# A router beside the experts: token ids from 10 + 4 matrix products instead of 40, and search products planned later

## The chip, the cores and the metric

The kernel runs on one core of a Trainium2 chip. A core has a tensor engine (PE; its weight loads are listed as PEld), a vector engine (DVE), a scalar engine (ACT), GpSimd (POOL) and a queue engine (SP) that only issues DMAs. Each executes its own instructions in the order in which they were written, and waits for the others by semaphores. The metric is the device time of one execution in microseconds.

## The reference

Attention over 8 batches of 8 heads (576 tokens, head size 64) with a bias from a running sum; its output is 4608 tokens of 512 numbers. Then a mixture of 8 experts: tokens and experts are paired greedily by descending logit, each expert takes 576 tokens, and each token passes through the two layers of its one expert.

```
logits = x @ w_gate                       # 4608 x 8
order = np.argsort(-logits.flatten())
for idx in order:
    tok, e = idx // E, idx % E
    if assigned[tok] >= 0 or counts[e] >= cap:
        continue
    assigned[tok] = e
    counts[e] += 1
for e in range(E):
    mask = assigned == e
    h = np.maximum(x[mask] @ w1[e], 0.0)
    out[mask] = h @ w2[e]
```

## The kernel before, in words

**Stages.** Attention comes first. After it come a router, which finds the greedy assignment without sorting, and the experts; the router's first search step (L886) starts at 358 us of the profiled execution. Router and experts are written into the same instruction streams.

**The router.** Tokens lie as 128 partitions by 40 columns. The router works in eight phases, j = 0 to 7; each settles which expert fills up next and which tokens go to it. Phases 0 to 6 search a threshold in seven steps, one digit of the key each. A step is a chain to and fro between DVE and PE: comparisons into `ge` (L886), ten products into `psa` that count per expert (L909), a copy `ca` (L913), four products into `psb` that add up over the partitions with the selecting matrices `qb` (L918), a comparison `pe` (L921), one product (L923), a maximum `jc` (L926), the next key `wd` (L930). Phase 7 has no search. Each phase then gives every chosen token its place among the 576 (products L982 and L983, a scan), and one product (L1003) updates the counts.

**Ids from places.** `Router.places` turns places into the list of token ids that the gather needs. A place is split into two digits of base 32 (`db`). `ol` marks for each token the lower digit (128 partitions, 10 groups, 32 values, 4 columns), `ob` the upper one (18 values). `rv` holds two factors of the id times `ob`: in its first half a number for the token's column, in its second the partition. Summing `ol` transposed times `rv` over all tokens leaves at [lower digit, upper digit] the id that has this place. The sum runs over 128 partitions and 40 columns; before, it is made of 40 products that accumulate, each with 32 columns of weights taken from `ol` at a step of 4 and 36 moving columns from `rv` at a step of 4. DVE copies the 32 x 36 sums to `pf` and makes `ids` of them. Then POOL gathers the expert's tokens (`xg`, L1097, five indirect DMAs), and SP transposes them by DMA (`xT`, L1104); for expert 0 PE does it (L1112).

**The experts.** Expert j has 96 large products in its first layer (512 columns, L1163), each with a short one behind it (64 columns, L1167), and 112 large ones in its second (L1237, L1234); for expert 0 the first layer is split and has more. ACT and DVE turn sums into `hT` and split each float32 weight, loaded by SP into `wst`, into a high part (ACT, L1132) and a low one (DVE, L1135). The loads start when the router has named the expert. Results go out by indirect DMAs of POOL (L1217).

**What sets the order.** A planner (`Plan`) takes tasks, each with an engine, a duration in microseconds, the tasks that it needs, a priority and the buffers that it takes. It simulates the engines with these durations and always writes out the task that could start first, lower priority number first among equals. A slot of a `Ring` of buffers comes free when the planned end of its last user has passed. The durations and `slack` are part of the kernel; they decide the order alone and make nothing wait at run time:

```
def _when(self, x, e):
    t = max(x.ready + x.slack, self.free[e])
```

Only the router's products inside `phase` carry slack, from the table `SLACK` by `min(j, 2)`: none in phase 0, 0.15 us in phase 1, 0.3 us in phases 2 to 7. The router's tasks have priority 0, the experts' products 2 + j. So the planner fills PE with expert products until a router product's planned time has come, and writes it there. At run time PE reaches it in that order, and if its operand is not there yet, PE waits with everything behind it.

Of the kernel before, what the change touches and what calls it, by code (L numbers as in the profile page):

```python
# [9 lines left out]
F32 = mybir.dt.float32  # L10
F16 = mybir.dt.float16
BF = mybir.dt.bfloat16
I32 = mybir.dt.int32
AF = mybir.ActivationFunctionType
# [10 lines left out]
CAP = 576  # L25
# [179 lines left out]
class Attention:  # L205
# [26 lines left out]
    def buf(self, name):  # L232
        return Buf(self.r[name])
# [465 lines left out]
WS1, WS2 = 32.0, 64.0  # L699
YSC = 1.0 / (VS * WS1 * WS2)  # L700
NEG = -1.0e30
SLACK = (0.0, 0.15, 0.3)
NONE = 1.0e9
NT = 8 * S

# [1 line left out]
class Router:  # L707
# [109 lines left out]
    def rings(self):  # L817
        w, o = self.w, self.out
        R = lambda pool, shape, dt, name, n: Ring([pool.tile(shape, dt, name=f"{name}{i}") for i in range(n)])
        self.r = dict(  # L820
            ge=R(w, [128, NC_ // 4, J, 4], F16, "ge", 2), y=R(w, [128, NC_], F32, "y", 2),
            ca=R(w, [128, 4, E], F16, "ca", 2), pe=R(w, [128, E], F16, "pe", 2), wd=R(w, [128, NC_], BF, "wd", 2),
            jc=R(w, [128, 8], F32, "jc", 2), jm=R(w, [128, 8], F32, "jm", 2), t8=R(w, [128, 7, E], F32, "t8", 2),
            gg=R(w, [128, 2, NC_], F32, "gg", 2), gv=R(w, [128, 2, NC_], F32, "gv", 2), vi=R(w, [128, 4], I32, "vi", 2),
            tm=R(w, [128, NC_, E], F32, "tm", 1), cp=R(w, [128, E], F16, "cp", 2),
            sel=R(w, [128, 2, E], F32, "sel", 2), v1=R(w, [1, 1], F32, "v1", 1), va=R(w, [128, E], F32, "va", 1),
            vstar=R(o, [128, 1], F32, "vstar", 3), ei=R(o, [1, 1], I32, "ei", 3),
            X=R(o, [128, 2, NC_], F16, "X", 3), Y=R(o, [128, 2, NC_], F32, "Y", 3), ids=R(o, [128, 5], I32, "ids", 4),
            Z=R(w, [128, 2, NC_], F32, "Z", 1), si=R(w, [128, NC_], I32, "si", 1), d=R(w, [128, 2, NC_], I32, "d", 1),
            db=R(w, [128, 2, NC_ // 4, 4], BF, "db", 1), ob=R(w, [128, NC_ // 4, CAP // 32, 4], BF, "ob", 1),  # L830
            rv=R(w, [128, 2, NC_ // 4, CAP // 32, 4], BF, "rv", 1), ol=R(w, [128, NC_ // 4, 32, 4], BF, "ol", 1),
            pf=R(w, [32, 2, CAP // 32], F32, "pf", 1),
            A=Ring([self.ps.tile([128, 512], F32, name="psa")]), B=Ring([self.ps.tile([128, 512], F32, name="psb")]),
            C=Ring([self.ps.tile([128, 512], F32, name="psc")]))

# [182 lines left out]
    def places(self, pl, info, X, Y, placed, prio):  # L1018

        nc, v = self.nc, self.nc.vector  # L1020
        buf = lambda name: Buf(self.r[name])
        chain = [placed]

        def V(dur, f, **k):
            chain[0] = pl.add("v", dur, f, chain[:1], prio=prio, **k)
            return chain[0]
        Z, si, d, db, ob, rv, ol, C, pf, ids = (buf(n) for n in ("Z", "si", "d", "db", "ob", "rv", "ol", "C", "pf", "ids"))
        nb = CAP // 32

        V(0.241, lambda: v.scalar_tensor_tensor(Z.t, Y.t, -1024.0, X.t, op0=OP.add, op1=OP.mult), takes=[Z], uses=[X, Y])  # L1030
# [15 lines left out]
              takes=[] if h else [ol], uses=[db] + ([ol] if h else []))  # L1046

        def f_pi():
            pi = C.t[0:32, 0:2 * nb].rearrange("p (a b) -> p a b", a=2)
            for q in range(10):  # L1050
                for c in range(4):
                    nc.tensor.matmul(pi, ol.t[:, q, :, c], rv.t[:, :, q, :, c], start=(q == c == 0),
                                     stop=(q == 9 and c == 3))
        chain[0] = pl.add("t", 1.25, f_pi, chain[:1], prio=prio, takes=[C], uses=[ol, rv])
        info["pi"] = chain[0]
        V(0.16, lambda: v.tensor_copy(pf.t, C.t[0:32, 0:2 * nb].rearrange("p (a b) -> p a b", a=2)), takes=[pf], uses=[C])
        for a in range(4):
            n = 5 if a < 2 else 4
            V(0.157, lambda a=a, n=n: v.scalar_tensor_tensor(
# [270 lines left out]
```

## Time and profile before

| | us |
|---|---|
| three runs, median | 839.58 |
| three runs, lowest and highest | 838.43, 843.65 |
| profiled execution, its own time | 842.17 |
| its span, first to last instruction | 840.3 |
| mean granted clock of PE over the span, share of full | 0.944 |
| busy: PE, DVE, ACT, POOL | 744.2, 606.2, 377.1, 349.7 |
| first and last of the products L1052 | 385.1, 681.0 |

An engine's busy time is the union of its instructions. A product counts as busy to its modelled end, about 0.17 us after the next one has started, so the time that a product takes in a stream is the distance between starts, or the time of a whole group in the chain of waits divided by its count. In the chain a row is a start, a time and a group that was on the chain. In the view in order of time a row is a start, a duration from the first start to the last end, the engine, the line, what is written and read, the shape and the count, and in square brackets the engine's idle time before it with what ended it. "issue" means that no wait that the profile shows ended then, "remote" a release that it cannot assign.

### The profile page before, as it was taken

Reading aid. Unit: us, or ns where it says so; the run is one execution under the profiler, and the core shown is the slowest. Engines: PE = TensorE matmul, PEld = TensorE weight load, DVE = VectorE, ACT = ScalarE, POOL = GpSimd, SP = SyncE. Lnnn points to the kernel's source line nnn. Section 1 sums busy time; section 2 is a strip of 40 time slices with the busy share of each in tenths; the row PEclk is TensorE's granted clock in tenths of the full one; section 3 lists DMA queues with packets and bytes.
Section 4 is the critical chain, followed back from the end, with each engine's and each line's share of the span. In section 5 each row is a group of like instructions: output and inputs, shape, how many; then the busy total and the mean of one; then the engine's idle time right before and its main releaser. Section 6 shows DMA issues by size and latency. Waiting matters only on the chain.

```text
span 840.3 us, 23577 instructions
## 1 busy us (share of the span) xinstructions
PE 744.2 (89%) x9267; PEld 470.0 (56%) x9267; DVE 606.2 (72%) x1992; ACT 377.1 (45%) x716; POOL 349.7 (42%) x423
## 2 busy tenths in 40 slices
PE   4299999999989999625999999998989999999995
PEld 1167778877768877512754545444545545454442
DVE  7679999999999997367887888886878854240110
ACT  2367877877768766403433323232323324231110
POOL 5178878878878887302023031222030150201011
PEclk7589999999999999856999999999999999999998
DMA  4956757675666511105258394848285494510001
GB/s 140 284 135 166 220 162 226 191 225 154 191 174 200 144 31 59 58 1 194 66 162 209 113 225 146 155 170 185 77 208 150 152 253 150 136 51 29 29 14 44
DMA packets 85317, 119.31 MB, mean 142 GB/s; under 512 B 40726, under 2 KB 57238, under 8 KB 85206
## 3 DMA queue, kind: packets, MB, share of 16 engines
q1 hardware_dynamic: 79318, 98.93, 42.5%
q0 software_dynamic: 5888, 18.88, 7.5%
q8 instruction: 72, 1.18, 0.6%
q14 instruction: 39, 0.32, 0.1%
HBM read 71.67 MB, written 19.10 MB: 108 GB/s over the span
## 4 chain that ended last, share of the span: by engine, by line
PE 43%; issue 21%; DVE 17%; POOL 4%; DMA 2%; another core or an unknown queue 1%; ACT 1%; POOLq 0%; DVEq 0%; SPq 0%; ACTq 0%
PE psm L1163 12%; PE psm L1237 9%; DVE scr L442 6%; DVE QK L381 3%; PE pst L514 2%; PE pst L515 2%; POOL out_dram L1217 2%; PE pss L473 2%; PE po L587 2%; PE po L589 2%; PE psn L1167 2%; PE po L588 2%; PE psa L909 2%; PE psm L1234 1%; POOL xg L1097 1%
## 5 line engine op out<-in xcount | busy, mean ns | idle before, releaser
L527 POOL TENSOR_TENSOR R<-P 128x512 f16<-128x512 f32 (+1 forms) x224 | 237.1, 1082 | 46.1 <-ACT P L525 44.9
L1163 PE MATMUL psm<-xT,w1p 128*128 128x512 f16 (+1 forms) x876 | 197.6, 356 | 0.0
L1237 PE MATMUL psm<-w2p,hT 128*128 128x512 f16 x768 | 175.9, 380 | 0.0
L1217 POOL DMA_INDIRECT out_dram<-y,ids x40 | 42.2, 1055 | 262.9 <-ACT y L1248 204.0
L1167 PE MATMUL psn<-xT,w1p 128*128 128x64 f16 x768 | 142.7, 193 | 0.0
L525 ACT ACTIVATE P<-pst 128x512 f32<-128x512 f32 (+1 forms) x224 | 117.7, 548 | 52.3 <-PE pst L517 25.6
L442 DVE CUSTOM_DVE_ANT_0 scr<-pss,mS 128x512 bf16<-128x512 f32 (+3 forms) x256 | 124.1, 485 | 13.6 <-PE pss L473 2.9
L1163 PEld LDWEIGHTS <-w1p 128*128 128x128 f16 x876 | 80.0, 98 | 83.9 <-issue 5.8
L1237 PEld LDWEIGHTS <-hT 128*128 128x128 f16 x768 | 70.2, 98 | 81.2 <-issue 3.2
L587 PE MATMUL po<-V,P 128*128 128x65 f16 x960 | 111.0, 196 | 2.3 <-DVE xp L608 1.8
L514 PE MATMUL pst<-QK 70*128 70x64 f16 (+4 forms) x512 | 106.7, 251 | 6.8 <-DMA QK<-mt 6.5
L589 PE MATMUL po<-V,R 128*128 128x65 f16 x960 | 111.0, 194 | 0.0
L588 PE MATMUL po<-Vl,P 128*128 128x64 f16 x960 | 110.8, 193 | 0.0
L515 PE MATMUL pst<-QK 128*128 128x64 f16 (+4 forms) x512 | 106.4, 251 | 0.0
L1097 POOL DMA_INDIRECT xg<-xs,ids x40 | 42.9, 1072 | 135.1 <-DVE w L809 43.6
L1183 ACT ACTIVATE hT<-psm 128x512 f16<-128x512 f32 x64 | 38.2, 597 | 133.9 <-PE psm L1163 99.2
L587 PEld LDWEIGHTS <-P 128*128 128x128 bf16 x960 | 90.2, 98 | 8.6 <-issue 6.1
L588 PEld LDWEIGHTS <-P 128*128 128x128 bf16 x960 | 89.7, 99 | 7.5 <-issue 3.7
L473 PE MATMUL pss<-QK 67*128 67x512 f16 (+3 forms) x256 | 73.4, 310 | 20.9 <-DVE mr L442 13.1
L589 PEld LDWEIGHTS <-R 128*128 128x128 f16 x960 | 89.7, 97 | 0.0
L1185 DVE SCALAR_TENSOR_TENSOR hT<-psm,hT 128x512 f16<-128x512 f32 x64 | 44.0, 687 | 51.6 <-ACT hT L1183 51.5
L1248 ACT ACTIVATE y<-psm 128x512 f32<-128x512 f32 x32 | 19.1, 597 | 130.2 <-PE psm L1237 121.0
(199 smaller groups left out, 1427.1 us busy)
## 6 DMA issues: line engine op xcount, KB each, us to landing
QK<-QK SPq DMA_DIRECT2D x120, 144.0 KB
wst<-in_w_dram SPq DMA_DIRECT2D x32, 512.0 KB
wst<-in_w_dram SPq DMA_DIRECT2D x64, 256.0 KB
rv<-in_v_dram SPq DMA_DIRECT2D x16, 576.0 KB
raw<-in_q_dram SPq DMA_DIRECT2D x15, 576.0 KB
raw<-in_k_dram SPq DMA_DIRECT2D x15, 576.0 KB
xs<-xp SPq DMA_DIRECT2D x8, 1024.0 KB
xs<-xp SPq DMA_DIRECT2D x8, 128.0 KB
```

The lines of the kernel that those rows point to most:

```text
L442: return pl.add("v", dur, lambda: nc.vector.tensor_tensor_reduce(scr.t[:, :n], ps(), mask, 1.0, init() if init else -3e38, OP.add, OP.max, ...
L473: nc.tensor.matmul(ps.t[:, :n], F()[:, q0:q0 + 128], F()[:, k0:k0 + n], start=True, stop=True)
L514: nc.tensor.matmul(ps[:, c0:c0 + n], F()[:, ks:ks + 128], F()[:, q:q + n], start=True, stop=False)
L515: nc.tensor.matmul(ps[:, c0:c0 + n], G()[:, ks:ks + 128], G()[:, q:q + n], start=False, stop=not diag)
L525: e = pl.add("a", n / 1200 + 0.171, lambda: nc.scalar.activation(P.t[:, c0:c0 + n], ps.t[:, :n], AF.Exp, scale=1.0 / YS), [x] + fresh, pri ...
L527: sub = lambda eng: eng.tensor_tensor(R.t[:, c0:c0 + n], P.t[:, c0:c0 + n], strided_hi(P.t)[:, c0:c0 + n], op=OP.subtract)
L587: nc.tensor.matmul(o[:, i], H[:, c:c + 128], V.t[:, pr, sl], start=f, stop=False)
L588: nc.tensor.matmul(o[:, i, 0:64], H[:, c:c + 128], Vl.t[:, pr, sl], start=False, stop=False)
L589: nc.tensor.matmul(o[:, i], R.t[:, c:c + 128], V.t[:, pr, sl], start=False, stop=l)
L1163: nc.tensor.matmul(ps[:, tiles[0]:tiles[-1] + 1] if len(tiles) > 1 else ps[:, tiles[0]], lhs(f, c, a), xT.t[:, tiles[0]:tiles[-1] + 1, 4 * ...
L1167: nc.tensor.matmul(pt.t[:, 64 * f:64 * f + 64], lhs(f, c, a), xT.t[:, 4, 4 * b + c, 0:64], start=s, stop=e)
L1237: nc.tensor.matmul(py.t, hT.t[:, f, a, 128 * i:128 * i + 128], w2p.t[:, f, b], start=f == 0 and k == 0, stop=f == 7 and k == 2)
```

## The change

`places` gets ten products in the place of forty. Each takes a whole group of four token columns: 128 columns of weights, which are 32 lower digits for each of the 4 columns, and 144 moving ones, which are 2 halves, 18 upper digits and 4 columns. Their sum also holds combinations of two different token columns, which mean nothing. ACT copies the 128 x 144 sums to float16 (`pc`, a new buffer). Then four products, one for each column of a group, select with 32 columns of `qb` the rows that belong to that column, take every fourth column of `pc`, and add the four up into 32 x 36 sums at another place of the same bank of PSUM. The planned durations are 0.63 us for the ten, 0.3 us for the copy and 0.12 us for the four, where the forty had 1.25 us. The third entry of `SLACK` goes from 0.3 to 0.45.

```diff
-SLACK = (0.0, 0.15, 0.3)
+SLACK = (0.0, 0.15, 0.45)
...
-            pf=R(w, [32, 2, CAP // 32], F32, "pf", 1),
+            pf=R(w, [32, 2, CAP // 32], F32, "pf", 1), pc=R(w, [128, CAP // 4], F16, "pc", 1),
...
         def f_pi():
-            pi = C.t[0:32, 0:2 * nb].rearrange("p (a b) -> p a b", a=2)
             for q in range(10):
-                for c in range(4):
-                    nc.tensor.matmul(pi, ol.t[:, q, :, c], rv.t[:, :, q, :, c], start=(q == c == 0),
-                                     stop=(q == 9 and c == 3))
-        chain[0] = pl.add("t", 1.25, f_pi, chain[:1], prio=prio, takes=[C], uses=[ol, rv])
+                nc.tensor.matmul(C.t[:, 0:8 * nb], ol.t[:, q].rearrange("p i c -> p (i c)"),
+                                 rv.t[:, :, q].rearrange("p a b c -> p a (b c)"), start=q == 0, stop=q == 9)
+        x = pl.add("t", 0.63, f_pi, chain[:1], prio=prio, takes=[C], uses=[ol, rv])
+        x = pl.add("a", 0.3, lambda: nc.scalar.activation(pc.t, C.t[:, 0:8 * nb], AF.Copy), [x], prio=prio, takes=[pc], uses=[C])
+
+        def f_pj():
+            for c in range(4):
+                nc.tensor.matmul(C.t[0:32, 256:256 + 2 * nb], self.qb[:, c, 0:32], pc.t.rearrange("p (x c) -> p x c", c=4)[:, :, c],
+                                 start=c == 0, stop=c == 3)
+        chain[0] = pl.add("t", 0.12, f_pj, [x], prio=prio, uses=[C, pc])
         info["pi"] = chain[0]
-        V(0.16, lambda: v.tensor_copy(pf.t, C.t[0:32, 0:2 * nb].rearrange("p (a b) -> p a b", a=2)), takes=[pf], uses=[C])
+        V(0.16, lambda: v.tensor_copy(pf.t, C.t[0:32, 256:256 + 2 * nb].rearrange("p (a b) -> p a b", a=2)), takes=[pf], uses=[C])
```

In the order of the changed kernel the lines from `places` on are renumbered: the wide products are L1051, the copy L1054, the four L1058, DVE's copy L1062, `ids` L1065, and the experts' L1132, L1135, L1163, L1167, L1183, L1185 and L1237 are L1138, L1141, L1169, L1173, L1189, L1191 and L1243.

PE at the end of phase 1, in the second layer of expert 0. Before, the first of the forty products stand directly behind the expert's, and the expert's follow the last (`psc` holds the sums):

```order
L1237 LDWEIGHTS hT_7635
L1237 MATMUL psm_7641<-w2p_7624,hT_7635 128x512
L1052 LDWEIGHTS ol_7611
L1052 MATMUL psc<-rv_7610,ol_7611 32x36
L1052 LDWEIGHTS ol_7611
```

PE at the same place now, from the last of the ten to the first of the four:

```order
L1051 LDWEIGHTS ol_7611
L1051 MATMUL psc<-rv_7610,ol_7611 128x144
L1243 LDWEIGHTS hT_7636
L1243 MATMUL psm_7642<-w2p_7625,hT_7636 128x512
L1243 LDWEIGHTS hT_7636
L1243 MATMUL psm_7642<-w2p_7625,hT_7636 128x512
L1243 LDWEIGHTS hT_7636
L1243 MATMUL psm_7642<-w2p_7625,hT_7636 128x512
L1058 LDWEIGHTS qb
L1058 MATMUL psc<-pc_7613,qb 32x36
```

Three large products of the expert stand between the two groups; it is so in phases 1 to 7 (in phase 0 nothing stands there).

ACT at the end of phase 4, before: the four conversions of the next expert's first weights (`w1p`) with results of an expert (`y`, `t`) between them:

```order
L1253 ACTIVATE t_7639<-psm_7643 64x512
L1132 ACTIVATE w1p_7622<-wst_7629 128x1024
L1132 ACTIVATE w1p_7622<-wst_7630 128x1024
L1248 ACTIVATE y_7637<-psm_7644 128x512
L1132 ACTIVATE w1p_7622<-wst_7626 128x1024
L1132 ACTIVATE w1p_7622<-wst_7627 128x1024
```

ACT at the same place now:

```order
L1138 ACTIVATE w1p_7623<-wst_7630 128x1024
L1189 ACTIVATE hT_7636<-psm_7643 128x512
L1138 ACTIVATE w1p_7623<-wst_7631 128x1024
L1138 ACTIVATE w1p_7623<-wst_7627 128x1024
L1054 ACTIVATE pc_7613<-psc 128x144
L1189 ACTIVATE hT_7636<-psm_7642 128x512
L1138 ACTIVATE w1p_7623<-wst_7628 128x1024
```

The new copy stands behind the third of the four conversions; so it does in phase 2, while in phases 1, 3, 5 and 6 it stands behind the second, and in phase 0 too.

DVE in the second step of the search of phase 5, before: from the key `y` to the maximum `jc`, with pieces of the experts' work (halves of a weight's low part, `hT`) between the links of the chain:

```order
L897 SCALAR_TENSOR_TENSOR y_7562<-wd_7568,dg 128x40
L1135 SCALAR_TENSOR_TENSOR w1p_7622<-wst_7630,w1p_7622 128x512
L913 CAST ca_7564<-psa 128x32
L1135 SCALAR_TENSOR_TENSOR w1p_7622<-wst_7630,w1p_7622 128x512
L921 TENSOR_TENSOR pe_7566<-psb,rem 128x8
L1185 SCALAR_TENSOR_TENSOR hT_7635<-psm_7643,hT_7635 128x512
L926 TENSOR_REDUCE jc_7571<-psb 128x1
```

DVE at the same place now:

```order
L897 SCALAR_TENSOR_TENSOR y_7562<-wd_7568,dg 128x40
L1141 SCALAR_TENSOR_TENSOR w1p_7623<-wst_7631,w1p_7623 128x512
L1141 SCALAR_TENSOR_TENSOR w1p_7623<-wst_7627,w1p_7623 128x512
L913 CAST ca_7564<-psa 128x32
L1141 SCALAR_TENSOR_TENSOR w1p_7623<-wst_7627,w1p_7623 128x512
L1141 SCALAR_TENSOR_TENSOR w1p_7623<-wst_7628,w1p_7623 128x512
L921 TENSOR_TENSOR pe_7566<-psb,rem 128x8
L1141 SCALAR_TENSOR_TENSOR w1p_7623<-wst_7628,w1p_7623 128x512
L1141 SCALAR_TENSOR_TENSOR w2p_7625<-wst_7629,w2p_7625 128x512
L926 TENSOR_REDUCE jc_7571<-psb 128x1
```

Two pieces of the experts' work stand between two links where one stood. On PE the distances grow alike. Counted in the experts' large products, the phases 2 to 6 end at products 387, 562, 731, 895 and 1062 before, and at 413, 611, 806, 1003 and 1200 now, of 1772 in all; phase 1 ends at 211 before and 214 now, phase 7 at 1117 and 1268. Experts 1 to 7 begin at products 316, 524, 732, 940, 1148, 1356 and 1564 in both.

More of the change, by code (lines that the diff above doesn't have):

```diff
@@ L1026, in V @@
             return chain[0]
-        Z, si, d, db, ob, rv, ol, C, pf, ids = (buf(n) for n in ("Z", "si", "d", "db", "ob", "rv", "ol", "C", "pf", "ids"))
+        Z, si, d, db, ob, rv, ol, C, pc, pf, ids = (buf(n) for n in ("Z", "si", "d", "db", "ob", "rv", "ol", "C", "pc", "pf", "ids"))
         nb = CAP // 32
```

## The prediction

> **What bounds the kernel now.** I read the page's slices first, then the busy time by stretch, then who waited for whom on the tensor engine, and last the order of time at one large wait. Of the page, PE is the tensor engine and PEclk its granted clock, in tenths:
>
> ```profile
> PE   4299999999989999625999999998989999999995
> PEclk7589999999999999856999999999999999999998
> ```
>
> A slice is 21 us. After the hole (6, 2, 5) PE is busy to the end; the hole is phase 0 of the router, which runs alone. The stretches (PE, PEld, DVE, ACT, POOL busy, clock, DMA):
>
> ```profile
> 353.00:386.00 33.00, 7.67 (x146) 5.40 (x144) 22.00 (x102) 1.53 (x2) 0.00 (x0) 0.51 0.21 71
> 404.00:692.00 288.00, 276.35 (x2532) 147.37 (x2530) 231.12 (x780) 91.12 (x142) 66.33 (x87) 0.99 0.61 163
> 692.00:738.00 46.00, 46.00 (x293) 22.25 (x292) 15.18 (x24) 15.81 (x26) 5.99 (x10) 1.00 0.47 139
> ```
>
> From 404 to 692 us seven phases of the router share PE with the experts, and PE is idle for 288.00 - 276.35 = 11.7 us; from 692 on only experts run, and it is not idle at all. So between 404 us and the end PE sets the time, and what leaves its queue comes off the span. Who waited for whom on PE from 404 us to 832 (total, times, longest):
>
> ```profile
> PE psb L918 <- DVE ca L913: 4.0, 2, 3.6
> PE psb L923 <- DVE pe L921: 2.6, 2, 1.9
> PE psb L923 <- issue: 1.9, 2, 1.2
> PE psb L918 <- issue: 1.2, 1, 1.2
> PE psa L982 <- POOL X L973: 1.1, 1, 1.1
> PE psa L909 <- DVE ge L886: 0.9, 2, 0.5
> ```
>
> That is all of the 11.7 us: ten waits, each ahead of a product of the router. The experts' products (L1163, L1167, L1234, L1237) are not in the list. They come in lumps; here is one, with the queue of SP and with DVE:
>
> ```profile
> 575.01 8.24 SPq L1104 DMA_TRANSPOSE xT<-xg  x4
> ...
> 575.83 0.19 DVE L913 CAST ca<-psa 128x32 f16<-128x32 f32 x1 [1.90 <-remote]
> 578.79 0.17 DVE L921 TENSOR_TENSOR pe<-psb,rem 128x8 f16<-128x8 f32 x1 [2.17 <-remote]
> ...
> 576.08 0.24 PE L918 MATMUL psb<-ca,qb 128*128 128x8 f16 x4 [1.24 <-issue]
> 576.18 0.38 PE L1163 MATMUL psm<-xT,w1p 128*128 128x512 f16 x1
> ...
> 576.42 0.38 PE L1163 MATMUL psm<-xT,w1p 128*128 128x512 f16 x1
> ...
> 579.01 0.17 PE L923 MATMUL psb<-pe,quart 128*128 128x8 f16 x1 [1.94 <-DVE pe L921]
> 579.04 0.59 PE L1163 MATMUL psm<-xT,w1p 128*128 128x512 f16 x1
> 579.42 0.26 PE L1167 MATMUL psn<-xT,w1p 128*128 128x64 f16 x1
> 579.49 0.61 PE L1163 MATMUL psm<-xT,w1p 128*128 128x512 f16 x1
> ```
>
> DVE's L921 starts 2.6 us after the products it reads (576.08), released by something that the profile cannot name, while SP's DMA transposes run; PE then waits in its turn. After it a pair of L1163 and L1167 takes 0.45 us (579.04 to 579.49) in place of 0.24 (576.18 to 576.42), since the clock is down:
>
> ```profile
> 578.70:582.10 3.40, 3.09 (x14) 1.37 (x14) 3.12 (x8) 0.60 (x1) 0.00 (x0) 0.51 1.21 175
> 629.90:633.40 3.50, 3.50 (x17) 1.35 (x14) 2.66 (x8) 1.11 (x2) 0.37 (x1) 0.51 1.07 282
> ```
>
> Two such stretches, each some 1.7 us lost.
>
> **The products of the ids.** Rows of the chain of waits and of PE in order of time:
>
> ```profile
> 403.78 1.81 PE psm L1163 x32
> 411.72 1.05 PE psn L1167 x36
> 430.21 1.54 PE psc L1052 x40
> ...
> 442.11 0.24 PE L918 MATMUL psb<-ca,qb 128*128 128x8 f16 x4
> 442.21 1.02 PE L1237 MATMUL psm<-w2p,hT 128*128 128x512 f16 x4
> ```
>
> Removed in each phase: 40 products of 36 columns, 1.54 us (38.5 ns each). Added: 10 products of 2 x 18 x 4 = 144 columns. The row of 32 with 128 columns gives 56.6 ns each, that of 36 with 64 columns 29.2, so a column costs 0.43 ns and 144 cost 63 ns: 0.63 us. Then 4 products of 36 columns, between 25 ns (L918, 442.11 to 442.21, of 8 columns) and 38.5 (the old ones, of 36 and strided too): 0.10 to 0.15; I take 0.15, its nearest row being the old one. Gain 1.54 - 0.63 - 0.15 = 0.76 us in each of the seven phases that share PE: 5.3 us. The group of four adds one more switch into and out of the experts' products; from nothing (442.21 follows 442.11 at 25 ns a product) up to one drain of 0.17 us (L923's busy time at 579.01), taken as 0.1 in each phase: 0.7 us back. DVE reads the ids' sums in the same shape as before, and neither SP nor POOL gets an instruction: their gathers, scatters, transposes and loads are the same ones, interleaved otherwise from phase 4 on, where expert 7 alone has loads between its transposes.
>
> By the Trainium skill (TensorE: Matmul & The Clock Gate, Back-to-back issue gap) a sustained stream of load and product holds about 81 ns at 128 columns; an estimate by that page is some 0.9 us for the ten and 3.5 us of gain. This trace's 56.6 ns, each with its own load, disagrees, and I go by the trace.
>
> **The copy between them.** It is new on ACT, of 144 elements. Nearest row:
>
> ```profile
> L497 ACT ACTIVATE mt<-pss 20x128 f16<-20x128 f16 x32 | 8.2, 255 | 3.7 <-PE pss L495 3.2 <-ACT P L525 0.5
> ```
>
> So 0.26 us. PE has three of the experts' products ahead of the second group: 0.65 to 0.73 us of cover, against about 0.17 (drain of the last wide product) + 0.26 + two hops of 0.05 (DVE's L921 ends at 578.96, L923 starts at 579.01). Hidden, if ACT is free. In the orders of phases 2 and 4 the copy stands behind the third conversion of an expert's first weights, elsewhere behind the second. Those conversions wait for DMAs. Phase 4 in the trace of before:
>
> ```profile
> 608.78 0.20 PE L982 MATMUL psa<-X,on 128*128 128x80 f16 x1
> ...
> 612.46 1.06 ACT L1132 ACTIVATE w1p<-wst 128x1024 f16<-128x1024 f32 x1 [0.65 <-DMA wst<-in_w_dram]
> 614.15 1.06 ACT L1132 ACTIVATE w1p<-wst 128x1024 f16<-128x1024 f32 x1 [0.64 <-DMA wst<-in_w_dram]
> 616.64 1.06 ACT L1132 ACTIVATE w1p<-wst 128x1024 f16<-128x1024 f32 x1 [1.43 <-DMA wst<-in_w_dram]
> ```
>
> The third ends 8.9 us after L982, the copy then at 9.3. In the new order 31 large products stand between L982 and the ids' products, in the first layer (0.245 us each with its short one): 7.6 + 0.63 + 0.73 = 9.0 us. So PE waits 0.3 us in those two phases; with as much again for late loads: 1.0 us back. ACT's own conversions move by 0.26 us, hidden by its idle time (91 of 288 us busy).
>
> **Phase 0.** It is a chain, not a stream, and PE's clock is at half there (0.51 above):
>
> ```profile
> 384.36 2.22 ACT L1132 ACTIVATE w1p<-wst 128x1024 f16<-128x1024 f32 x2 [31.57 <-DMA wst<-in_w_dram]
> 385.12 1.60 PE L1052 MATMUL psc<-rv,ol 128*32 128x36 bf16 x40 [2.75 <-DVE ol L1044]
> 387.07 0.18 DVE L1056 COPY pf<-psc 32x36 f32<-32x36 f32 x1
> ```
>
> The forty end at 386.7. Ten wide ones at half clock take 10 x 0.12 = 1.2 and end, drained, near 386.5; ACT is free at 386.6, the copy ends at 386.9, four products and their drain bring 387.3 to 387.4: the ids come 0.3 us later (nothing to 0.8), and expert 0 with them.
>
> **The later products.** SLACK touches phases 2 and on: a search product is planned 0.45 and not 0.3 us after what it needs. By the order a digit takes some 19 large products of the experts, not 17: mostly 5 ahead of L918, 4 ahead of L923 and 10 ahead of the next L909, where 4, 4 and 9 stood. So a signal may be one product (0.22 us) later before PE stands. In each of the ten waits that is 2.2 us. Below, it may be nothing, since the next digits meet the transposes at other places; above, all 11.7. I take 2.2, and 1.0 for the clock, as one of two half-clock stretches may go (0 to 3.4).
>
> What is late next: a phase now lasts 195 to 199 large products, not 164 to 176, and the last ids come at product 1268 of 1772, not 1117. The tightest phases keep 102 to 111 before their expert (before: 105 in phase 1), at 0.22 us or more 22 us. Phase 1 shows the need:
>
> ```profile
> 446.90 1.21 SPq L1104 DMA_TRANSPOSE xT<-xg  x1
> ...
> 457.72 0.38 PE L1163 MATMUL psm<-xT,w1p 128*128 128x512 f16 x1
> ```
>
> Its last transpose is issued 11 us ahead of its expert, so nothing starves.
>
> **Sum.** -5.3 + 0.7 + 1.0 + 0.3 - 2.2 - 1.0 = -6.5 us. The profiled execution took 842.17 us, so 835.7. The median of the three runs, 839.58, is 2.6 lower (they run from 838.43 to 843.65); from it 833.1 follows. I forecast between the two: **834.5**.
>
> **Rivals.** *The late signals only move* (0.25): up to 3.6 us long, they are not covered by one product, and the next ones fall elsewhere. Then only -5.3 + 0.7 + 1.0 + 0.3 = -3.3 is left: 838.9 by the profiled run, 836.3 by the median. For it: of the lump shown, 1.24 and 1.94 us, 0.22 is little. *Most lumps go* (0.15): fewer digits meet each gather. With half of 11.7 and both half-clock stretches gone: -3.3 - 5.9 - 3.4 = -12.6, so 829.6 or 827.0. Against it: every phase still has its gather and transposes close behind its ids. By the Trainium skill (TensorE: Matmul & The Clock Gate, What's actually happening) the clock halves after an idle window of about 3.4 us; the trace agrees in length, 3.40 and 3.50 us at 0.51. *The copy turns into PE's wait* (0.08), the side of slower: behind a conversion that ends at 617.70 as in the row above, with the ids' products where they were (615.23 + 0.63 + 0.65 = 616.5), the second group starts at 618.1, a wait of 1.6 us. In six phases 9.4 in place of 1.0: 844.1, or 841.5. It decides from a mean of 1.25 us a phase on. *The weights bound the wide product* (0.05): a load of 128 columns is not hidden.
>
> ```profile
> L1163 PEld LDWEIGHTS <-w1p 128*128 128x128 f16 x876 | 80.0, 98 | 83.9 <-issue 5.8
> ```
>
> Ten loads at 98 ns make 0.98 us, 0.35 more in each phase: 838.1, or 835.5. The skill's 81 ns lies on this side; the 56.6 ns speak against it. That the products do not go is excluded by the order.
>
> **Numbers.** The forecast holds 0.47. The range 827.5 to 841.0 takes in the forecast, late signals, wide product, and the nearer halves of the other two. Under 1% is about what a measurement of this kernel cannot tell from no change: 831.2 to 848.0. Faster takes most of the lumps' 0.15 and a fifth of the forecast's 0.47: 0.24. Slower needs the copy to wait 2.2 us or more in each phase: 0.04. Same: 0.72.
>
> **What would show it.** The ids' products: ten in about 0.63 us and four in 0.15, in eight phases; no idle time over 0.3 us ahead of the four; PE's idle time between 404 us and the last ids near 9 to 10 us; the experts' first layers with no wait. Wrong, if ACT's copy is released by a weight's DMA, if the ten take 0.9 us, or if the half-clock stretches grow in number.

## The result and the profile after

| | before | changed |
|---|---|---|
| median of five runs, us | 842.04 | 829.24 |
| lowest and highest | 838.43, 843.82 | 827.57, 835.8 |
| ratio of the times, 95% interval | | 0.9853 [0.9814, 0.9891] |
| profiled execution | 842.17 | 835.8 |

The changed kernel is faster by 12.8 us at the medians. Its profiled execution is the slowest of its five runs, so its trace shows only half of that, 6.4 us. Two delays in it come first, since they hide a part of what the other runs gained.

The page's slices of the changed kernel:

```profile
PE   5288999999989999624999999999999799999995
PEclk8599999999999999855799999999999999999998
```

PE is busy from the end of phase 0 on, as before. The clock, though, is still down when the experts begin (5, 5, 7). Busy time by stretch, for the changed kernel (columns as before: PE, PEld, DVE, ACT, POOL, clock, DMA):

```profile
404.00:692.00 288.00, 278.37 (x2388) 146.68 (x2387) 214.94 (x727) 91.47 (x147) 55.59 (x75) 0.98 0.56 147
...
399.50:403.00 3.50, 3.22 (x45) 2.81 (x43) 3.13 (x9) 2.59 (x5) 0.00 (x0) 0.50 0.05 16
403.00:407.00 4.00, 4.00 (x53) 4.00 (x51) 2.51 (x8) 1.80 (x4) 0.00 (x0) 0.57 0.55 174
```

The first delay is a half clock in the first 7 us of the experts. In the trace of before the same stretch has:

```profile
399.50:403.00 3.50, 2.39 (x47) 1.79 (x43) 2.92 (x9) 3.29 (x5) 0.00 (x0) 1.00 0.28 82
```

At a clock of 0.50 and 0.57 for 7.5 us some 3.5 us are lost. The idle time of PE between 404 and 692 us is 288.00 - 278.37 = 9.6 us, where it was 11.7. Who waited for whom on PE from 404 to 832 us in the changed kernel:

```profile
PE psa L909 <- DVE ge L886: 4.8, 1, 4.8
PE psb L918 <- DVE ca L913: 2.6, 2, 1.9
PE psb L923 <- DVE pe L921: 2.0, 2, 1.5
```

Five waits stand where ten stood, but one of 4.8 us is new, and it is the second delay. Here it is in order of time, with SP's queue:

```profile
657.21 1.22 SPq L1110 DMA_TRANSPOSE xT<-xg  x1
658.69 4.57 SPq L1134 DMA_DIRECT2D wst<-in_w_dram  x6
659.47 0.63 ACT L1138 ACTIVATE w2p<-wst 128x512 f16<-128x512 f32 x1 [7.98 <-DMA wst<-in_w_dram]
660.13 0.69 DVE L1141 SCALAR_TENSOR_TENSOR w2p<-wst,w2p 128x512 f16<-128x512 f32 x1 [5.94 <-ACT w2p L1138]
...
661.21 0.82 DVE L886 TENSOR_TENSOR ge<-wd,kj 128x1280 f16<-128x1280 bf16 x1
...
662.09 0.42 PE L909 MATMUL psa<-oh,ge 128*128 128x32 f16 x10 [4.82 <-DVE ge L886]
```

A weight lands late, ACT waits 7.98 us for it, and DVE behind ACT 5.94 us. The router's next key stands behind that piece of weight on DVE's queue and the comparison `ge` behind the key, so PE stands 4.8 us for a weight that it needs only much later. A second profile of the same kernel (below) does not have this wait, but a shorter one of the same kind at another place.

The products themselves, in phases 0, 1 and 4 of the changed kernel:

```profile
382.90 1.38 PE L1051 MATMUL psc<-rv,ol 128*128 128x144 bf16 x10 [2.75 <-DVE ol L1044]
...
383.63 1.06 ACT L1138 ACTIVATE w1p<-wst 128x1024 f16<-128x1024 f32 x1 [0.19 <-DMA wst<-in_w_dram]
...
384.60 0.27 ACT L1054 ACTIVATE pc<-psc 128x144 f16<-128x144 f32 x1
...
384.92 0.30 PE L1058 MATMUL psc<-pc,qb 128*32 128x36 f16 x4 [0.64 <-ACT pc L1054]
...
385.32 0.18 DVE L1062 COPY pf<-psc 32x36 f32<-32x36 f32 x1 [0.39 <-PE psc L1058]
...
430.79 0.79 PE L1051 MATMUL psc<-rv,ol 128*128 128x144 bf16 x10
...
431.41 0.81 PE L1243 MATMUL psm<-w2p,hT 128*128 128x512 f16 x3
...
431.95 0.29 ACT L1054 ACTIVATE pc<-psc 128x144 f16<-128x144 f32 x1 [0.47 <-PE psc L1051]
...
432.29 0.30 PE L1058 MATMUL psc<-pc,qb 128*32 128x36 f16 x4
...
432.52 0.82 PE L1243 MATMUL psm<-w2p,hT 128*128 128x512 f16 x3
...
584.78 2.19 ACT L1138 ACTIVATE w1p<-wst 128x1024 f16<-128x1024 f32 x2 [0.80 <-DMA wst<-in_w_dram]
...
586.87 0.27 ACT L1054 ACTIVATE pc<-psc 128x144 f16<-128x144 f32 x1
...
587.36 0.30 PE L1058 MATMUL psc<-pc,qb 128*32 128x36 f16 x4
```

In phase 1 the ten take 431.41 - 430.79 = 0.62 us and the four 432.52 - 432.29 = 0.23, to the start of the next product. In phase 4 the copy does end its wait behind a weight's conversion, yet the four have no idle time ahead of them. In phase 0, where no expert's products lie between, PE waits 0.64 us for it. In phase 1 the three large products just fail to cover it: they end at 432.22, the copy at 432.24, and the four start at 432.29.

### The profile page after: what moved, and what is told of

It reads as the page before. It is cut to its first block, busy times and chain, and to the rows that moved or that the text cites. A ratio compares the mean times of both kernels' runs of the same rounds, so it can differ in the third digit from the quotient of the medians.

```text
span 834.1 us, 23171 instructions
## 1 busy us (share of the span) xinstructions
PE 740.5 (89%) x9059; PEld 466.9 (56%) x9059; DVE 605.6 (73%) x1992; ACT 379.8 (46%) x724; POOL 348.1 (42%) x423
## 2 busy tenths in 40 slices
DMA packets 85316, 119.30 MB, mean 143 GB/s; under 512 B 40726, under 2 KB 57238, under 8 KB 85206
## 4 chain that ended last, share of the span: by engine, by line
PE 44%; issue 18%; DVE 17%; DMA 5%; POOL 4%; ACT 1%; another core or an unknown queue 0%; SPq 0%; POOLq 0%; DVEq 0%; ACTq 0%
PE psm L1169 13%; PE psm L1243 10%; DVE scr L442 6%; DVE QK L381 3%; PE pst L514 2%; DMA xg<-xs,ids 2%; PE pst L515 2%; PE pss L473 2%; PE psm L1240 2%; PE psn L1173 2%; PE psa L909 2%; PE po L587 2%; POOL out_dram L1223 2%; PE po L589 2%; PE po L588 1%
## 5 line engine op out<-in xcount | busy, mean ns | idle before, releaser
L1169 PE MATMUL psm<-xT,w1p 128*128 128x512 f16 (+1 forms) x876 | 197.4, 358 | 0.0
L1243 PE MATMUL psm<-w2p,hT 128*128 128x512 f16 x768 | 178.5, 383 | 0.0
L1173 PE MATMUL psn<-xT,w1p 128*128 128x64 f16 x768 | 142.2, 193 | 0.0
L1169 PEld LDWEIGHTS <-w1p 128*128 128x128 f16 x876 | 81.8, 100 | 80.1
L1243 PEld LDWEIGHTS <-hT 128*128 128x128 f16 x768 | 70.3, 98 | 81.1 <-issue 5.4
L1189 ACT ACTIVATE hT<-psm 128x512 f16<-128x512 f32 x64 | 38.2, 597 | 119.1 <-PE psm L1169 94.8
L1173 PEld LDWEIGHTS <-w1p 128*128 128x128 f16 x768 | 72.8, 98 | 0.7
```

The source lines that it names most:

```text
L1169: nc.tensor.matmul(ps[:, tiles[0]:tiles[-1] + 1] if len(tiles) > 1 else ps[:, tiles[0]], lhs(f, c, a), xT.t[:, tiles[0]:tiles[-1] + 1, 4 * ...
L1173: nc.tensor.matmul(pt.t[:, 64 * f:64 * f + 64], lhs(f, c, a), xT.t[:, 4, 4 * b + c, 0:64], start=s, stop=e)
L1243: nc.tensor.matmul(py.t, hT.t[:, f, a, 128 * i:128 * i + 128], w2p.t[:, f, b], start=f == 0 and k == 0, stop=f == 7 and k == 2)
```

## The experiments

There were three sessions on chips, and each times its kernels against its own runs of the kernel before. Those medians of before differ a great deal: 842.04 us with the result, then 846.61, 840.51 and 826.87. Times are therefore compared inside a session only. In diffs, what stands against the changed kernel is shown, if nothing else is said.

**First session (before: 846.61 us, 842.27 to 851.01, 11 runs): the parts of the change.** The products alone:

```diff
-SLACK = (0.0, 0.15, 0.45)
+SLACK = (0.0, 0.15, 0.3)
```

> The change with the third entry of SLACK back at 0.3: the products alone. In the profile of the changed kernel the ids take 0.63 + 0.23 us of PE in place of 1.54 in each of seven phases, 4.8 us less, and phase 0 is 0.3 to 0.5 us later. Theory A (the two parts add up, and the slack is worth the rest of the 12.8 us): 4 to 5 us faster than before, ratio 0.995. Rival B (the slack is worth nothing, the rest came from where the orders happen to place the waits): the waits ahead of search products stay at some 12 us in the profile, and the time may be anywhere from 4 to 13 us faster.

836.9 us, ratio 0.9893 [0.9860, 0.9926]: 9.7 us faster, about twice what Theory A gave. PE's idle time is 10.4 us in this kernel (table at the end of this section), so most of the waits stayed, as rival B had it.

The later plan alone (against the kernel before; the forty products stay):

```diff
-SLACK = (0.0, 0.15, 0.3)
+SLACK = (0.0, 0.15, 0.45)
```

> The kernel before with the third entry of SLACK at 0.45: the later plan alone, forty products. Theory A: 7 to 9 us faster than before, ratio 0.990 to 0.992, with PE's waits ahead of the router's products between 404 us and the last ids clearly under the 11.7 us of before. Rival B: 0 to 2 us faster, waits near 11.7.

831.76 us, ratio 0.9838 [0.9807, 0.9869]: 14.9 us faster, more than either expectation allowed. The longest waits on PE in this kernel with forty products and the later plan:

```profile
PE psb L918 <- DVE ca L913: 3.3, 3, 1.7
PE psb L923 <- DVE pe L921: 1.9, 3, 1.0
```

And its busy time from the first to the last of the experts' large products:

```profile
396.11:818.69 422.58, 415.37 (x3454) 217.14 (x3452) 265.24 (x838) 129.62 (x204) 82.80 (x115) 1.00 0.51 135
```

PE stands 422.58 - 415.37 = 7.2 us in all, and the longest wait is 1.7 us. The changed kernel once more, unchanged:

> The changed kernel once more, beside the other three on one chip: ratio 0.981 to 0.989 as in the result. Its profile is a second sample: if the 5 us wait ahead of L909 near 657 us of the first profile is an accident of that execution, it is absent here and the span is some 5 us shorter.

828.4 us, ratio 0.9773 [0.9746, 0.9801], under the range expected. Its waits on PE, without the wait of 4.8 us for `ge`:

```profile
PE psb L918 <- DVE ca L913: 4.7, 3, 2.1
PE psb L923 <- DVE pe L921: 2.4, 2, 1.6
PE psb L918 <- issue: 0.2, 1, 0.2
```

And its stage of the experts, in which PE stands 8.4 us:

```profile
399.34:818.73 419.39, 410.97 (x3273) 211.28 (x3270) 265.19 (x838) 131.14 (x211) 81.40 (x115) 1.00 0.49 136
```

One of these waits, in phase 4, is of the kind of the 4.8 us:

```profile
556.53 0.63 ACT L1138 ACTIVATE w2p<-wst 128x512 f16<-128x512 f32 x1 [7.74 <-DMA wst<-in_w_dram]
...
557.20 0.69 DVE L1141 SCALAR_TENSOR_TENSOR w2p<-wst,w2p 128x512 f16<-128x512 f32 x1 [3.32 <-ACT w2p L1138]
...
558.04 0.24 PE L918 MATMUL psb<-ca,qb 128*128 128x8 f16 x4 [2.14 <-DVE ca L913]
```

ACT waits 7.74 us for a weight, DVE waits behind ACT, and the search's copy `ca` stands behind that piece on DVE's queue. So the 4.8 us were not an accident of one execution. Waits in which the search stands behind a weight on DVE's queue are in the trace of the later plan alone (1.6 us) and in all three of the changed kernel (5.3, 2.1 and, in the third session, 1.0 us). They are in none of the four traces with 0.3 for all links (before twice, the products alone, and a kernel below whose search starts 7 us later), and in the one with more margin at two links (last experiment) they come to 2.4 us. So they look like a price of the later plan.

The four medians of the first session make a square:

| us | SLACK 0.3 | SLACK 0.45 | plan's part |
|---|---|---|---|
| forty products | 846.61 | 831.76 | -14.9 |
| ten and four | 836.90 | 828.40 | -8.5 |
| products' part | -9.7 | -3.4 | |

The parts don't add up: 9.7 + 14.9 = 24.6 us, and together they give 18.2. A likely reading is that each part alone moves the search's products on PE to other places and so changes what waits, and that this can be won only once. There is no trace of the kernel before from the first session to show it. On the plan where few waits are left the products are worth 3.4 us. The plan is the larger part here, by 8.5 or 14.9 us.

More of the same, `SLACK` 0.6:

```diff
-SLACK = (0.0, 0.15, 0.45)
+SLACK = (0.0, 0.15, 0.6)
```

> The changed kernel with the third entry of SLACK at 0.6. Theory A (each 0.15 us planned gives one large product more of cover): a further 1 to 4 us faster than the changed kernel, ratio to before 0.981 to 0.984. Rival B: no different from the changed kernel within 0.4%. A third outcome, slower than the changed kernel, would say that the router's chain has come too close to the experts that wait for its ids.

834.28 us, ratio 0.9851 [0.9822, 0.9880]: worse than 0.45. Its waits on PE (rows left out):

```profile
PE psb L918 <- DVE ca L913: 7.9, 5, 1.9
PE psn L1173 <- DMA xT<-xg: 1.2, 1, 1.2
```

A phase is now 208 to 210 of the experts' large products long, and an expert has 208. Five of its six late releases (counted as said below) come at 446, 500, 556, 610 and 663 us, one in each phase, at the same link, and make five waits on L918 where there were two or three. And the first wait of an expert for its transposed tokens appears.

**Second session (before: 840.51 us, 837.12 to 846.95, 17 runs): where the waits come from.** The kernel before again, for its trace:

> The kernel before once more, for a second profile of it. The runs beside the four experiments had a median of 846.6 us where the first profile had 842.2. If waits make the difference, PE's idle time between 404 us and the last ids, 11.7 us in the first profile, or the half-clock stretches, two there, are larger here whenever the time is; attention, up to the first search step at 357.7 us, stays within 3 us.

840.02 us. Its largest waits on PE:

```profile
PE psb L918 <- DVE ca L913: 5.1, 3, 3.4
PE psb L923 <- DVE pe L921: 2.6, 2, 2.3
```

In order of time, the lump that the prediction showed in the first trace of before:

```profile
573.81 0.19 DVE L913 CAST ca<-psa 128x32 f16<-128x32 f32 x1 [1.86 <-remote]
...
574.06 0.24 PE L918 MATMUL psb<-ca,qb 128*128 128x8 f16 x4 [1.21 <-DVE ca L913]
...
577.10 0.17 DVE L921 TENSOR_TENSOR pe<-psb,rem 128x8 f16<-128x8 f32 x1 [2.50 <-remote]
...
577.21 0.60 ACT L1183 ACTIVATE hT<-psm 128x512 f16<-128x512 f32 x1 [5.88 <-remote]
577.32 0.17 PE L923 MATMUL psb<-pe,quart 128*128 128x8 f16 x1 [2.27 <-DVE pe L921]
```

It is the same product, and the waits are 1.21 and 2.27 us where the prediction's rows had 1.24 and 1.94. So a given order has its waits at given places. The rows also say what a wait is: the products L918 end near 574.3, DVE then stands for 2.50 us with L921 next, and yet L921 starts at 577.10. ACT, waiting for other sums of PE, starts within 0.11 us of it. The trace also records when PE raised its semaphore: three times in a row, at 577.07, 577.13 and 577.18 us, for products whose modelled ends are 574.30, 574.78 and 575.05. So it is PE's signals that came late here, to two engines at once, and not DVE or ACT that were slow to start. That PE's work was done by then rests on the modelled ends and on PE having gone on to later products.

To count these, a release is called late here where DVE's L913, L921 or L926 starts more than 0.3 us after both the end of the product that it reads and the end of DVE's instruction before it. Each trace has 115 to 120 such links from 404 us on. Both traces of before have 12, and eleven of them are at the same link of the same step and phase. The changed kernel has five in the result's trace and eight in that of the first session, and all five are among the eight.

Whether the DMA transposes make the signals late: the next kernel has none, since PE transposes the tokens of every expert, as it did for expert 0.

```diff
-    def expert(self, pl, j, info, behind=None, ident=None):
+    def expert(self, pl, j, info, behind=None, ident=None, split=False):
...
-        split = ident is not None
...
-        behind = M.expert(pl, j, info, behind, R.ident16 if j == 0 else None)
+        behind = M.expert(pl, j, info, behind, R.ident16, j == 0)
```

> The changed kernel with every expert's tokens transposed on PE, as expert 0's are, with no DMA transposes. It adds 40 products of some 56 ns, 2.2 us, and five evacuations on ACT of about 1 us to each of seven experts, so PE has 15 us more to do. Theory T (the waits of over 1 us come from the DMA transposes beside the gather): no wait of over 1 us ahead of L909, L918 and L923 in the phases 2 to 7, and PE's idle time there in sum under 4 us. Rival G (the gather alone, or the order of DVE, makes them): lumps of 1 to 4 us stay, some 7 to 10 us in sum.

858.42 us in one run. The largest waits on PE in this kernel:

```profile
PE psm L1118 <- DMA xg<-xs,ids: 6.9, 7, 2.4
PE psb L923 <- DVE pe L921: 4.6, 3, 1.8
```

And one lump of it in order of time:

```profile
645.73 1.94 ACT L1120 ACTIVATE xT<-psm 128x1024 f16<-128x1024 f16 x2 [4.69 <-remote]
645.78 0.17 DVE L921 TENSOR_TENSOR pe<-psb,rem 128x8 f16<-128x8 f32 x1 [2.28 <-remote]
...
646.00 0.17 PE L923 MATMUL psb<-pe,quart 128*128 128x8 f16 x1 [1.83 <-DVE pe L921]
```

It is slower since PE has the transposes (L1118) and waits for gathers. But there are still six late releases of 0.8 to 2.3 us, and in two of them ACT is released at the same moment as DVE. Theory T is refuted: the DMA transposes are not needed for late signals.

Next, `SLACK` as before, but the first product of each search from phase 2 on is planned 7 us later, past the gather:

```diff
-SLACK = (0.0, 0.15, 0.45)
+SLACK = (0.0, 0.15, 0.3)
...
-        def T(dur, f, deps=None, **k):
-            x = pl.add("t", dur, f, chain[:1] if deps is None else deps, prio=prio, slack=SLACK[min(j, 2)], **k)
+        def T(dur, f, deps=None, late=0.0, **k):
+            x = pl.add("t", dur, f, chain[:1] if deps is None else deps, prio=prio, slack=SLACK[min(j, 2)] + late, **k)
...
-                T(0.28, f_pa, takes=[A], uses=[ge])
+                T(0.28, f_pa, late=7.0 if s == 0 and j > 1 else 0.0, takes=[A], uses=[ge])
```

> The changed kernel with SLACK back at 0.3 and, in phases 2 to 6, the first search product planned 7 us later, so that by its order 53 to 57 large products stand between the ids and the first search product and not some 20. The transposes run some 4 to 13 us after the ids, the search starts at about 12 us. Cover inside the search is as before the change (4, 4 and 9 large products). Theory P (where the search meets the gather and the transposes makes the waits): idle time ahead of search products falls to under 4 us and the time is 3 to 8 us under that of the products alone with SLACK 0.3, ratio to before 0.980 to 0.986. Rival C (the cover between two links makes them): no faster than the products alone, ratio 0.987 to 0.993.

831.98 us, ratio 0.9902 [0.9882, 0.9923]. Its waits on PE are one row:

```profile
PE psb L918 <- DVE ca L913: 8.4, 5, 2.2
```

One wait in each of five phases, and not under 4 us in all: Theory P is refuted, and the ratio lies in rival C's range. The transposes had moved later too, so the search met the gather and them after all, in four of the five phases at the same link. Then the same with 0.45 (the last two changes without the first):

> The changed kernel, SLACK 0.45, with the same 7 us ahead of the first search product. Theory P: no better than the last one within 0.4%, and 0 to 4 us under the changed kernel, ratio 0.973 to 0.980. Rival C: the changed kernel's time within 0.4%, ratio 0.977 to 0.981. If the phases, now as long as an expert, make experts wait for their tokens, it is slower than the changed kernel, and the profile has waits of L1169 for xT.

841.81 us in 12 runs, ratio 1.0011 [0.9987, 1.0035]: the whole gain is gone, which neither range allowed. The first of its waits on PE:

```profile
PE psb L918 <- DVE ca L913: 5.8, 7, 2.9
PE psb L923 <- DVE pe L921: 3.5, 2, 1.8
```

Idle time is 15.0 us from 404 to 832 us, more than in the kernel before. A phase is 208 large products long here too, and in phases 3 to 6 the order has one step of the search whose L918 and L923 follow with no product of an expert between, where four to six stand in nearly all other steps. At that step PE stands 7.4 of the 15.0 us, and none of this kernel's six late releases is at it: there PE waits for the bare chain and for the pieces of weights on DVE's queue. Later is not safer in itself: what counts is what stands between two links.

**Third session (before: 826.87 us, 822.90 to 831.05, 23 runs).** It was to find which traffic makes the signals late: the experts' weights, or the gathers. The record gives chip 7 for the first session and chip 8 for the second and the third, so the chip's number does not tell the third from the others. The weights of experts 2 to 7 are not loaded:

```diff
-            ld = pl.add("s", 0.65, lambda: nc.sync.dma_start(
-                st.t[:, :n], src[bass.ds(which[0], 1), 128 * key:128 * key + 128, :].rearrange("e p f -> p (e f)")),
-                [tw], prio=prio, takes=[st], lat=self.LAND, kb=n / 2)
+            def load():
+                if j < 2:
+                    nc.sync.dma_start(st.t[:, :n], src[bass.ds(which[0], 1), 128 * key:128 * key + 128, :].rearrange("e p f -> p (e f)"))
+            ld = pl.add("s", 0.65, load, [tw], prio=prio, takes=[st], lat=self.LAND, kb=n / 2)
```

> The changed kernel without the loads of the weights of the third expert and on (its conversions read what the buffers held); gathers, transposes and results stay. Theory D (the late releases come when gather, transposes and weight loads fill the DMA engines): no wait over 0.5 us ahead of L909, L918 and L923 in the phases 3 to 7, PE's idle time after 500 us under 2 us. Rival: lumps of 0.7 to 2.2 us as in the two profiles of the changed kernel, 2.5 to 7 us after 500 us; then the loads have no part in it.

823.44 us in one run. And plain copies of rows in order by SP in place of the gathers of experts 1 to 7:

```diff
-                in_offset=bass.IndirectOffsetOnAxis(ap=ids.t[:n, i:i + 1], axis=0)), [ti], prio=1,
+                in_offset=bass.IndirectOffsetOnAxis(ap=ids.t[:n, i:i + 1], axis=0)) if j == 0 else nc.sync.dma_start(
+                xg.t[:n, i], self.xs[CAP * j + 128 * i:CAP * j + 128 * i + n]), [ti], prio=1,
```

> The changed kernel with the tokens of experts 1 to 7 fetched by plain DMAs of SP, rows in order and not the chosen ones, in place of POOL's indirect gather; transposes, loads and results stay. Theory G (POOL's gather of scattered rows is what makes releases late): no wait over 0.5 us ahead of L918 and L923 in the phases 2 to 7. Rival D (any full DMA engines): lumps of 0.7 to 2.2 us stay wherever the DMA share is near 1.

815.76 us in one run. Neither has a late release; neither does the changed kernel itself, run beside them:

> The changed kernel on the chip of the last one: ratio between 0.975 and 0.988, the two seen so far, and a third profile: waits of 7 to 10 us ahead of the router's products, one or two half-clock stretches from 404 us to 800.

823.67 us, ratio 0.9968 [0.9948, 0.9988]: nearly no gain, and none of the waits expected. All its waits on PE from 404 us on:

```profile
PE psb L918 <- DVE ca L913: 0.6, 1, 0.6
PE psb L923 <- DVE pe L921: 0.5, 1, 0.5
```

And its stage of the experts:

```profile
398.00:808.17 410.17, 408.33 (x3271) 211.29 (x3269) 265.50 (x838) 132.16 (x211) 81.64 (x115) 1.00 0.50 139
```

This is the same program as in the first session, with the same DVE busy time (265.50 against 265.19 us) and the same traffic (85316 DMA packets and 119.30 MB in each trace); PE does not stand 8.4 us in it but 1.8. Both waits above are behind a weight. So the two kernels with less traffic say nothing on the cause: in the third session there was nothing to take away.

Last, the early plan with a margin only where the waits were:

```diff
-SLACK = (0.0, 0.15, 0.45)
+SLACK = (0.0, 0.15, 0.3)
...
-        def T(dur, f, deps=None, **k):
-            x = pl.add("t", dur, f, chain[:1] if deps is None else deps, prio=prio, slack=SLACK[min(j, 2)], **k)
+        def T(dur, f, deps=None, more=0.0, **k):
+            x = pl.add("t", dur, f, chain[:1] if deps is None else deps, prio=prio, slack=SLACK[min(j, 2)] + (more if j > 1 else 0.0), **k)
...
-                T(0.11, f_pb, takes=[B] if s == 0 else (), uses=[ca] + ([B] if s else []))
+                T(0.11, f_pb, more=0.15, takes=[B] if s == 0 else (), uses=[ca] + ([B] if s else []))
```

The line of L923 gets `more=0.15` in the same way.

> The changed kernel with SLACK at 0.3 and 0.15 more for L918 and L923 alone, the second and third product of a search step: by its order mostly 5 and 5 large products ahead of them, as with 0.45, but phases of 188 to 195 large products. If cover inside a step is what counts (9.7 of the 11.7 us of waits before stood there), it equals the changed kernel within 0.4%, ratio 0.973 to 0.985. If the longer phases as a whole count, it falls between the products alone (0.989) and the changed kernel.

823.69 us, ratio 0.9961 [0.9939, 0.9982]: the same as the changed kernel. Without late signals that does not decide between the two expectations; how it does where signals come late was not tried. No experiment that leaves nothing out beats the changed kernel.

**The traces side by side.** All but that of the kernel that transposes on PE, whose PE has other work. From the first to the last of the experts' large products, in stretches of 2 us: idle is the length less PE's busy time, clock is the length times what the granted clock lacks to 1, and the rest is what is left of the stage.

| kernel | session | stage, us | idle | clock | rest | late releases |
|---|---|---|---|---|---|---|
| before | of the result | 430.1 | 12.6 | 3.4 | 414.1 | 12 |
| before again | second | 429.1 | 12.1 | 3.4 | 413.6 | 12 |
| plan alone | first | 422.6 | 7.2 | 1.7 | 413.7 | 5 |
| products alone | first | 422.6 | 10.4 | 4.3 | 407.8 | 10 |
| changed | of the result | 424.7 | 9.9 | 6.9 | 407.9 | 5 |
| changed again | first | 419.4 | 8.4 | 1.7 | 409.3 | 8 |
| `SLACK` 0.6 | first | 422.0 | 11.3 | 1.7 | 409.0 | 6 |
| search 7 us later, 0.3 | second | 419.9 | 9.5 | 1.7 | 408.7 | 7 |
| search 7 us later, 0.45 | second | 432.7 | 15.3 | 6.8 | 410.7 | 6 |
| no loads from expert 2 on | third | 408.8 | 1.0 | 0.1 | 407.7 | 0 |
| plain copies for gathers | third | 410.1 | 0.9 | 1.7 | 407.5 | 0 |
| margin at two links | third | 413.2 | 4.3 | 0.3 | 408.6 | 0 |
| changed again | third | 410.2 | 1.8 | 0.3 | 408.0 | 0 |

The rest falls into two groups: 413.6 to 414.1 with forty products, 407.5 to 410.7 with ten and four, with means of 413.8 and 408.5. So the products are worth some 5 us of PE's work wherever they are run. All else is idle time and clock, and that is a matter of the plan and of the session.

## Why the prediction was right, and which term was not

829.24 us lies inside the range and 5.3 us below the forecast of 834.5. Both terms of the sum are there, the products and some of the waits, but not in the order forecast: the sum had -4.6 us for the products and -3.2 for the later plan with the clock, and in the first session the plan is the larger part. The result is almost that of the rival in which most lumps go (829.6 from the profiled time). That it lies inside the range is in part luck. Of the 12.8 us some 2.5 come from the median of before, which was 839.58 for the forecast and is 842.04 with five runs; and the ratio of the first session, applied to 842.04, would have given 822.9, outside.

- *The products, -5.3 + 0.7 = -4.6.* Seven phases save 1.54 - 0.63 - 0.23 = 0.68 us each: -4.8. The ten were right; the four take 0.23 to the start of the next product, not 0.15, and those 0.08 are the switch, which had been set at 0.1. That the weights would bound the wide product is refuted: ten in 0.625 us are 62.5 ns each. By the Trainium skill (TensorE: Matmul & The Clock Gate, Back-to-back issue gap) a stream of load and product holds 81 ns at 128 columns; here 144 columns take less, as in the row that the prediction went by.
- *The wait for the copy, +1.0.* It did not come in phases 2 to 7, and in phase 1 it was 0.07 us, though the copy stands where the order put it, and in phase 4 behind a conversion that had waited for its weight (rows above). Three large products cover it but for that. The rival built on it (844.1) falls with it.
- *Phase 0, +0.3.* From the first of the ids' products to DVE's copy it took 385.32 - 382.90 = 2.42 us, where 387.07 - 385.12 = 1.95 stood: +0.5.
- *These fixed terms, -3.3.* Where late signals were absent the change measures 826.87 to 823.67, which is -3.2 us, and on the later plan of the first session the products' part is -3.4. That is the size of the sum as predicted, and of the first rival's. The agreement is partly luck: the terms as measured make -4.8 + 0.5 = -4.3, since the 1.0 for the copy did not come, and the third session's interval, -4.3 to -1.0 us, holds both.
- *The later products, -2.2, and the clock, -1.0.* This is the step that failed, in size. What the result has beyond the measured -3.2 is -12.8 + 3.2 = -9.6 us. The prediction priced the margin at one large product in each of ten waits that stay where they are. But the order of a phase moves as a whole, and with it how many links meet a late signal at all: where there are late releases, 10 to 12 are counted on the early plan (before twice, products alone) and 5 to 8 on the later one (plan alone, changed twice). PE's waits that a late release explains fall from 10.2 us in the first trace of before to 4.1 in the result's. Against that stands a term that the sum did not have, the search held by a weight: nothing before, 5.3 us in the result's trace, 2.1 in the second. The clock gave nothing back in the result's trace, where 6.9 us are lost to it and 3.4 were before; in the second it is 1.7. (The 3.40 and 3.50 us that the prediction compares are the lengths of half-clock stretches; its rows do not show how long PE had been idle ahead of them.) The bounds of the term, nothing to 11.7 us with 3.4 for the clock, did hold both cases: nearly all of it in the first session, and, by the total alone, nothing in the third.
- *The experts' first layers without wait.* Right at 0.45. At 0.6 the first one appears (L1173, 1.2 us), since the phases have grown to an expert's length.
- *The idle time between 404 us and the last ids, 9 to 10 us.* The trace has 9.6, by luck: 4.8 of it is the late weight. It had not been seen that the search hangs on a weight's arrival, through DVE's queue.

Not predicted at all was that the gain depends on the session. The kernel before spans 19.7 us between sessions (826.87 to 846.61), the changed one 5.6 (823.67 to 829.24). An estimate of what late signals cost, with the third session's medians as a floor, is 13.6 to 19.7 us for the kernel before and 4.7 to 5.6 for the changed one; it puts the whole difference between sessions down to them, and there is no trace of the kernel before from the third session. So the plan's gain is to be read as less sensitivity to late signals: its ratio is 0.9773 in one session, 0.9968 in another, and in none of the three sessions that timed it was it slower than before.

What makes the signals late stays open. Shown is that one order meets them at nearly the same products in two sessions, that PE's semaphore is raised late, so that ACT, where it waits too, gets the signal with DVE, that DMA transposes are not needed, and that a session can be without them while the program and its traffic are the same. That gathers or loads play a part is argued only from where the lumps lie; the two kernels made to test it ran in the quiet session and could not tell. A test would need them run beside the kernel before in a session in which that kernel takes 840 us.

## What to carry to other kernels

When a stream shares an engine with a chain of small dependent steps, price the instructions removed and the margin of the chain apart: the first is steady, the second depends on how late signals come in that session, here from about nothing (third session, by the sum alone) to more than the first. Measure such a change in more than one session and against the kernel before in each; one session gave 0.997 here and another 0.977. Give the chain a margin, but keep a round of it shorter than a round of the stream: in the orders whose phases were as long as an expert, the same collision came back in nearly every phase. And look at what else stands in the queues of the chain's other engines, since with the later plan the search came to stand behind weights on DVE's.

## What the runs showed of the hardware

- Releases of DVE and ACT by finished products came 0.3 to 4.8 us late in 5 to 12 of some 117 links of DVE in three sessions, and in none in a fourth. The changed kernel, the same program each time, had 5, 8 and none. In the lump at 577 us PE's semaphore went up three times within 0.1 us, 2.1 to 2.8 us after the products' modelled ends.
- The clock was halved after stretches in which PE was not quiet: in the kernel before, run again, 3.4 us with PE busy for 1.00 us of them stand ahead of 6.8 us at 0.50 to 0.51, of which the second row below has the first half.

```profile
573.00:576.40 3.40, 1.00 (x10) 0.55 (x10) 0.79 (x2) 0.00 (x0) 2.08 (x4) 1.00 0.85 206
576.40:579.80 3.40, 2.48 (x12) 1.10 (x12) 2.67 (x8) 0.60 (x1) 0.00 (x0) 0.51 1.23 198
```

- From their first start to their last end the forty small products took 1.60 us at a granted clock of 0.50 (phase 0, the prediction's row) and 1.59 to 1.61 us at 1.00 (phases 1 to 7), some 36 ns from start to start in both: the granted clock did not set their time. The ten wide ones took 0.79 us at 1.00 (phase 1) and 1.38 us at 0.50 (phase 0).
